# Two more token tiles transposed by the DMA queue, and a new written order for the first stage of a fused adaLN, linear attention and GLU kernel

## The chip, the cores and the metric

The kernel runs on one core of a Trainium2 chip. It is written for five instruction streams: PE (TensorE, matmuls and their weight loads), DVE (VectorE), ACT (ScalarE), POOL (GpSimd) and SP (SyncE, which here only issues DMAs). The metric is the device time of one execution in microseconds; the profile gives the span from the first to the last instruction of one profiled execution.

## What is computed

The input x has 2048 tokens of width D = 512; c is one row of 512. In the reference's words, cut short:

```python
mod = (silu(c) @ w_mod)                      # six rows: sa, ca, ga, sb, cb, gb
h = layernorm(x) * (1 + ca) + sa
q, k, v = split(h @ wqkv)                    # 32 heads of 16
phi(t) = concat(softmax(t @ w_phi), softmax(-t @ w_phi))    # per head, 32 features
kv = sum over tokens of phi(k)^T v ;  z = sum over tokens of phi(k)
o = (phi(q) @ kv) / (phi(q) @ z + 1e-6)
x = x + ga * (o @ wo)
h = layernorm(x) * (1 + cb) + sb
x = x + gb * ((sigmoid(h @ w_gate) * (h @ w_up)) @ w_down)  # F = 1376
```

The sum kv needs all 2048 keys before the first numerator phi(q) @ kv can be formed.

## The kernel before

The tokens stand in 16 tiles of 128. Everything before the first numerator is called the first stage here, everything from it on the second.

**First stage, per tile t.** `st1_t` (DVE, L702 and L703) takes mean and variance of a tile of x. `rs1_g` (ACT or POOL) and `nmr1_g` (DVE, L718) make the scale and shift for the tiles of a group g; `LG` lists the groups: tiles 0 and 1 alone, then pairs, so group 4 is tiles 6 and 7, and group 5 is tiles 8 and 9. `xn1_t` (POOL L731, ACT L727, DVE L729) writes the normalised tile in bf16. It must then be transposed, in four blocks of 128 features, and modulated with the columns of `modc` (1 + ca, sa). There are two ways:

- `TD[g] = 0`: PE transposes the block into a PSUM bank (`tph` with group and block, L744, into the tile named tp_h), and `hm1` with group and block (L751 on ACT, L753 on DVE) reads PSUM and writes the block of `h1T`. POOL has no part in this way.
- `TD[g] = 1`: SP issues a DMA transpose for each tile (`xT1_t`, L736) straight into `h1T`, and `hm1` modulates it in place on ACT, POOL or DVE.

Then `K` (L817), `V` (L821) and `Q` (L871) are matmuls of four 128x512 pieces each; K of the first 8 and V of the first 4 tiles are split in halves a and b. K and Q use `wqk_f`, weights with w_phi folded in (`tpw`, `wTc`, `fold`, `foldc`), V uses `wv_sb`, loaded by the one DMA `ld_wv0` (L551). Per key tile follow `e` (ACT, exponentials, L776), `n` (DVE, sums, L780), `r` (reciprocal: DVE L798, or ACT as logarithm and exponential, L794 and L795), `phi` (POOL or DVE, L787), `va` (ACT, L836) and `kv` (PE, L282, accumulates over all tiles). Query tiles have `qe`, `qn`, `qphi` and a DMA transpose `pT` likewise. At the end `kvz`, `kvn` (DVE, L299 and L294) mask the sums and `num0a` (PE, L326) is the first numerator.

**Second stage.** Per tile: numerators, reciprocal, output projection (a_ps), second LayerNorm, then gate, up and down projections (g_ps, u_ps, y_ps) in chunks of up to four tiles.

**What sets the order.** The schedule is manual. A long string `ORDER` names every task once; the instructions of each engine are issued in the order in which its tasks stand there, and every engine and the SP queue work in order. A letter behind `@` picks the engine (A for ACT, P for POOL, D for DVE); without one, the first of the task's list stands, which for `hm1` is DVE with `TD = 0` and ACT with `TD = 1`, for `r` and `qphi` DVE, for `foldc` ACT, for `phi` POOL. Buffers (8 PSUM banks, 7 slots for e and phi, and so on) are handed out in the same order, so a new order also changes who waits for whose buffer.

## Time and profile before

| | |
|---|---|
| three timed runs | 202.9, 204.34 and 409.55 us; median 204.34 us |
| the profiled execution | 203.25 us; span 201.3 us; granted TensorE clock 1.00 |
| busy: PE, DVE, ACT, POOL | 193.6, 160.0, 104.9, 103.9 us |
| first numerator (num0a) starts | 56.5 us |
| bytes read and written in HBM | 11.58 and 2.10 MB |

One of the three runs took twice the time of the others, so the median is the higher of the two that agree. The profiled execution lies between these two; 1.95 us of it are outside the span. In the profile, times count from the start of the span, and PE matmuls are shown with their pipeline, so that neighbouring rows overlap: what PE takes for a piece of work is read from start to start.

### The profile page before, as it was taken

How to read it: one execution, taken by the hardware profiler on the slowest of the kernel's cores; microseconds unless marked ns; L12 is line 12 of the kernel's file. 1: busy time of each engine (PE TensorE's matmuls, PEld its weight loads, DVE VectorE, ACT ScalarE, POOL GpSimd, SP SyncE). 2: the span in 40 equal slices, each digit the busy share in tenths (PEclk: the TensorE clock that was granted, in tenths of full speed). 3: DMA queues.
4: the chain of work that ended last, by engine and by line, in shares of the span. 5: the costliest groups of instructions: out<-in, count | busy, mean ns of one | idle time of the engine just before them, and what ended most of it. 6: DMA issues, size and time to landing. Idle time of an engine off the chain costs nothing.

```text
span 201.3 us, 4128 instructions
## 1 busy us (share of the span) xinstructions
PE 193.6 (96%) x1447; PEld 106.1 (53%) x1471; DVE 160.0 (79%) x376; ACT 104.9 (52%) x250; POOL 103.9 (52%) x146
## 2 busy tenths in 40 slices
PE   7889999999999999999999999999999999999993
PEld 2555665455565777668744444444444444444442
DVE  3999999999999999997997796875969662326632
ACT  2899999999978974486621215312112420334100
POOL 4889978887899998876660166130030332000000
PEclk9999999999999999999999999999999999999999
DMA  5999956729964883455573334442113031000011
GB/s 163 336 292 236 295 204 126 113 62 268 396 248 78 133 111 68 85 34 105 104 80 80 70 62 102 84 110 56 25 25 74 2 78 55 26 8 26 28 55 55
DMA packets 49453, 22.94 MB, mean 114 GB/s; under 512 B 38065, under 2 KB 47634, under 8 KB 49426
## 3 DMA queue, kind: packets, MB, share of 16 engines
q1 hardware_dynamic: 48896, 22.59, 48.8%
q8 instruction: 13, 0.21, 0.4%
q14 instruction: 14, 0.11, 0.2%
q10 hardware_dynamic: 530, 0.02, 0.1%
HBM read 11.58 MB, written 2.10 MB: 68 GB/s over the span
## 4 chain that ended last, share of the span: by engine, by line
PE 64%; DVE 26%; issue 5%; ACT 2%; DMA 1%; DVEq 0%
PE y_ps L485 19%; PE u_ps L447 18%; PE g_ps L447 18%; DVE ks L780 6%; PE a_ps L356 5%; DVE st L702 5%; DVE qks L780 3%; DVE phi L787 3%; DVE kr L798 2%; PE num L326 2%; DVE h1T L753 2%; DMA x_sb<-in_A_x_dram 1%; DVE mv L703 1%; PE g_ps L449 1%; DVE nmr L718 1%
## 5 line engine op out<-in xcount | busy, mean ns | idle before, releaser
L457 ACT ACTIVATE tg<-g_ps 128x512 bf16<-128x512 f32 (+5 forms) x66 | 28.7, 455 | 66.6 <-PE g_ps L447 39.7
L468 DVE SCALAR_TENSOR_TENSOR wmod_sb<-tg,u_ps 128x512 bf16<-128x512 bf16 (+4 forms) x63 | 30.2, 491 | 18.1 <-ACT tg L457 11.5
L485 PE MATMUL y_ps<-wd_sb,wmod_sb 128*128 128x512 bf16 (+4 forms) x180 | 44.2, 366 | 0.2
L447 PEld LDWEIGHTS <-wg_sb 128*128 128x128 bf16 (+1 forms) x252 | 21.9, 99 | 16.1 <-issue 0.2
L447 PEld LDWEIGHTS <-wu_sb 128*128 128x128 bf16 (+1 forms) x252 | 21.7, 99 | 15.9 <-issue 0.2
L784 POOL TENSOR_TENSOR qphi<-qe,qks 128x512 bf16<-128x512 bf16 x24 | 25.2, 1066 | 3.9 <-DMA pT<-qphi 1.6
L485 PEld LDWEIGHTS <-wmod_sb 128*128 128x128 bf16 (+1 forms) x187 | 17.1, 98 | 16.0 <-issue 0.6
L447 PE MATMUL u_ps<-wT_sb,wu_sb 128*128 128x512 bf16 (+2 forms) x124 | 23.8, 322 | 0.1
L447 PE MATMUL g_ps<-wT_sb,wg_sb 128*128 128x512 bf16 (+2 forms) x122 | 23.0, 321 | 0.2
L447 PE MATMUL g_ps<-wqk_sb,wg_sb 128*128 128x128 bf16 (+4 forms) x127 | 19.9, 286 | 0.1
L447 PE MATMUL u_ps<-wqk_sb,wu_sb 128*128 128x128 bf16 (+4 forms) x127 | 19.8, 286 | 0.1
L492 DVE TENSOR_TENSOR ot<-y_ps,x 128x512 bf16<-128x512 f32 (+2 forms) x17 | 11.1, 654 | 10.4 <-PE y_ps L485 10.3
L780 DVE TENSOR_REDUCE ks<-e 128x64 f32<-128x1024 bf16 (+2 forms) x22 | 19.2, 901 | 0.0
L780 DVE TENSOR_REDUCE qks<-qe 128x64 bf16<-128x1024 bf16 x16 | 19.1, 1202 | 0.0
L376 POOL TENSOR_SCALAR ve<-mv 128x2 f32<-128x2 f32 (+1 forms) x8 | 1.8, 225 | 33.3 <-DVE mv L366 33.2
L776 ACT ACTIVATE e<-k_ps 128x512 bf16<-128x512 f32 (+2 forms) x44 | 18.2, 519 | 0.0
L776 ACT ACTIVATE qe<-q_ps 128x512 bf16<-128x512 f32 x32 | 17.0, 611 | 0.8 <-POOL phi L787 0.5
L817 PE MATMUL k_ps<-wqk_f,h1T 128*128 128x512 bf16 x61 | 16.0, 379 | 0.1
L787 POOL TENSOR_TENSOR phi<-e,kr 128x1024 bf16<-128x1024 bf16 (+2 forms) x10 | 14.8, 1484 | 2.6 <-DVE phi L787 1.2
L356 PE MATMUL a_ps<-wo_sb,oT 128*128 128x512 bf16 x60 | 15.9, 379 | 0.2
L871 PE MATMUL q_ps<-wqk_f,h1T 128*128 128x512 bf16 x61 | 15.7, 379 | 0.1
L821 PE MATMUL v_ps<-wv_sb,h1T 128*128 128x512 bf16 x61 | 15.4, 379 | 0.1
(132 smaller groups left out, 305.6 us busy)
## 6 DMA issues: line engine op xcount, KB each, us to landing
out_dram<-ot SPq DMA_DIRECT2D x15, 128.0 KB, 1.7
x_sb<-in_A_x_dram SPq DMA_DIRECT2D x6, 256.0 KB, 4.7
wmod_sb<-in_w_mod_dram SPq DMA_DIRECT2D x1, 1536.0 KB, 7.0
wu_sb<-in_B_w_up_dram SPq DMA_DIRECT2D x1, 1376.0 KB, 11.5
wg_sb<-in_B_w_gate_dram SPq DMA_DIRECT2D x1, 1376.0 KB, 11.9
wd_sb<-in_B_w_down_dram SPq DMA_DIRECT2D x1, 1280.0 KB, 8.5
wmod_sb<-in_w_mod_dram SPq DMA_DIRECT2D x4, 256.0 KB, 6.1
wqk_sb<-in_A_wqkv_dram SPq DMA_DIRECT2D x2, 256.0 KB, 4.4
```

Of the source, the lines that this page charges most:

```text
L356: pe.matmul(ap_[:], lhsT=oT[:, j, :], rhs=wo_sb[:, j, :], start=(j == 0), stop=(j == KT - 1))
L447: pe.matmul(ps[:fsz, 0:n], lhsT=w[:, j, ft * P:ft * P + fsz], rhs=h[:, j, 0:n], start=(j == 0), stop=(j == KT - 1))
L457: G.add(f"tg{k}.{ft}", {"ACT": 0.13 + n * 0.00083}, lambda e, tg=tg, g_ps=g_ps, fsz=fsz, n=n: act.activation(tg[:fsz, 0:n], g_ps[:fsz, 0:n ...
L468: dve.scalar_tensor_tensor(hm_all[:fsz, hm[k].slot, ft, 0:n], tg[:fsz, 0:n], 1.0, u_ps[:fsz, 0:n], op0=ALU.add, op1=ALU.mult)
L485: mm = pe.matmul(y[:, 0:c1 - c0], lhsT=hm_all[:fsz, hm[k].slot, ft, tl * P:(tl + 1) * P], rhs=wd_sb[:fsz, ft, c0:c1], start=(ft == 0), sto ...
L776: act.activation(ee[:, a:b, s].rearrange("p g f h -> p g (f h)"), kp[:, a * 64:b * 64].rearrange("p (g n) -> p g n", n=64), ACT.Exp, scale ...
L780: dve.tensor_reduce(ks[:, a:b].rearrange("p g s h -> p (g s) h"), ee[:, a:b].rearrange("p g s f h -> p (g s) h f"), axis=AX.X, op=ALU.add)
L784: engine(e).tensor_tensor(ph[:].rearrange("p (g s f h) -> p g s f h", s=2, f=DH, h=4)[:, :, s], ee[:, :, s], ks[:, :, 1 - s].unsqueeze(2). ...
L787: engine(e).tensor_tensor(ph[:, a * P:b * P].rearrange("p (g f h) -> p g f h", f=DH, h=4), ee[:, a:b].rearrange("p g s f h -> p (g s) f h" ...
L817: pe.matmul(kp[:], lhsT=h1T[:, j, t * P:(t + 1) * P], rhs=wqk_f[:, j, D:2 * D], start=(j == 0), stop=(j == KT - 1))
L821: pe.matmul(vp[:], lhsT=h1T[:, j, t * P:(t + 1) * P], rhs=wv_sb[:, j, :], start=(j == 0), stop=(j == KT - 1))
L871: pe.matmul(qp[:], lhsT=h1T[:, j, t * P:(t + 1) * P], rhs=wqk_f[:, j, 0:D], start=(j == 0), stop=(j == KT - 1))
```

## The change

Two things change, and both lie in the first stage. Group 5 (tiles 8 and 9) gets `TD = 1`: its eight PE transposes into four PSUM banks go, two DMA transposes `xT1_8` and `xT1_9` on SP come, and of its four modulated blocks two move to POOL (`hm1_51@P`, `hm1_52@P`) and two go to ACT. And the part of `ORDER` ahead of `num0a` is written anew, with other engines for some tasks; from `num0a` on, the string is the same word for word. The SP queue keeps the order of its first 23 DMAs, up to the loads of the other modulation weights and of wo; xT1_9 and xT1_8 come behind these. The diff, cut to the table and to the first lines of the string:

```diff
-TD = [0, 0, 0, 0, 0, 0, 1, 1, 0]
+TD = [0, 0, 0, 0, 0, 1, 1, 1, 0]
...
-hm1_00@A tph02 hm1_23 rs1_6@P hm1_13@A hm1_02 nmr1_3 st1_9 st1_8 xn1_5 tph03 K0a tph41 hm1_03@A tph40 xn1_4 K2a hm1_22@A hm1_12@A hm1_41@A hm1_40 wqT1 nmr1_6
...
+hm1_20@A K3a modc1c1 nmr1_3 hm1_03@A st1_10 hm1_41 V0a st1_9 hm1_02@A xn1_5 tph42 tph43 wqT3 tph23 hm1_12@A hm1_13@A rs1_6@P hm1_42 xn1_4 nmr1_6 xn1_10 st1_8
...
```

Tasks of the first stage that change their engine (beside group 5):

| from | to | tasks |
|---|---|---|
| ACT | DVE | hm1_01, hm1_41, hm1_42, foldc01, r0, r2, r4, r5, r7, the second half of r14 |
| DVE | ACT | hm1_02, hm1_23, hm1_33, hm1_81, r1, r6, r8, modc1c1 |
| POOL | DVE | one half of qphi0, one half of qphi4, a quarter of phi11 |
| DVE | POOL | phi3, a quarter of phi11 |
| ACT, POOL | the other of the two | xn1_3 (to POOL), rs1_3 and hm1_72 (to ACT) |

**PE, where the first matmul with the V weights stands.** In the rows, `LDWEIGHTS` loads a block, v_ps is the result of V, k_ps that of K, tp_h a transposed block; the first V is V0a, tile 0. Before, the rows around it are the last three pieces of K of tile 1, V0a, and one transposed pair of group 4:

```order
L817 MATMUL k_ps_434<-wqk_f_67,h1T_73 128x512
L817 LDWEIGHTS h1T_73
L817 MATMUL k_ps_434<-wqk_f_67,h1T_73 128x512
L821 LDWEIGHTS h1T_73
L821 MATMUL v_ps_461<-wv_sb_66,h1T_73 128x512
L821 LDWEIGHTS h1T_73
L821 MATMUL v_ps_461<-wv_sb_66,h1T_73 128x512
L744 LDWEIGHTS xn_321
L744 MATMUL tp_h_468<-ident_75,xn_321 128x128
```

Now on PE, at the same V0a, a half of K of tile 3 stands ahead of it, and two blocks of group 4 (tp_h_375 is the one of `tph42`) behind it:

```order
L817 MATMUL k_ps_356<-wqk_f_67,h1T_73 128x512
L817 LDWEIGHTS h1T_73
L817 MATMUL k_ps_356<-wqk_f_67,h1T_73 128x512
L821 LDWEIGHTS h1T_73
L821 MATMUL v_ps_367<-wv_sb_66,h1T_73 128x512
L821 LDWEIGHTS h1T_73
L821 MATMUL v_ps_367<-wv_sb_66,h1T_73 128x512
L744 LDWEIGHTS xn_348
L744 MATMUL tp_h_375<-ident_75,xn_348 128x128
L744 LDWEIGHTS xn_322
L744 MATMUL tp_h_375<-ident_75,xn_322 128x128
```

V0a has moved forward past six halves of K (of tiles 0 to 3), one fold and eight pairs of transposes, among them the block of `tph42`, which now stands right behind it.

**DVE, in the middle of the statistics.** BN_STATS and BN_AGGR are one `st1`; h1T<-tp_h is an `hm1` from PSUM, nmr an `nmr1`. Before, from `modc1c1` to the twelfth `st1` and the block `hm1_40`:

```order
L638 TENSOR_TENSOR modc_78<-modc_ps_332,mone_80 128x2x2
L753 TENSOR_SCALAR h1T_73<-tp_h_309,modc_78 128x256
L753 TENSOR_SCALAR h1T_73<-tp_h_355,modc_78 128x128
L718 TENSOR_SCALAR nmr_89<-mv1_82,rs1_84 128x1 x2
L702 BN_STATS st1_81<-x_sb_65 128x6
L703 BN_AGGR mv1_82<-st1_81 128x2
L702 BN_STATS st1_81<-x_sb_65 128x6
L703 BN_AGGR mv1_82<-st1_81 128x2
L753 TENSOR_SCALAR h1T_73<-tp_h_379,modc_78 128x256
```

Now on DVE, from the second `nmr1` pair of the same stretch to the one behind `hm1_42`, which reads tp_h_375:

```order
L718 TENSOR_SCALAR nmr_89<-mv1_82,rs1_84 128x1 x2
L702 BN_STATS st1_81<-x_sb_65 128x6
L703 BN_AGGR mv1_82<-st1_81 128x2
L753 TENSOR_SCALAR h1T_73<-tp_h_350,modc_78 128x256
L702 BN_STATS st1_81<-x_sb_65 128x6
L703 BN_AGGR mv1_82<-st1_81 128x2
L753 TENSOR_SCALAR h1T_73<-tp_h_375,modc_78 128x256
L718 TENSOR_SCALAR nmr_89<-mv1_82,rs1_84 128x1 x2
```

Two blocks of group 4 that ACT modulated are DVE's now; the second stands on DVE behind eleven `st1`, where before `hm1_40` stood behind twelve, and it reads a PSUM block that PE writes behind V0a.

## The prediction

> **What bounds the kernel now.** I looked first at the page, then at the busy time of the engines in four stretches: the start, the first stage up to the last key work, the passage to the second stage, and the rest.

> ```profile
> PE 193.6 (96%) x1447; PEld 106.1 (53%) x1471; DVE 160.0 (79%) x376; ACT 104.9 (52%) x250; POOL 103.9 (52%) x146
> ...
> core 0: us, PE busy (x) PEld busy (x) DVE busy (x) ACT busy (x) POOL busy (x), PEclk, DMA share, GB/s
> 0.00:12.60 12.60, 10.21 (x85) 5.17 (x86) 9.18 (x31) 8.34 (x21) 8.57 (x30) 1.00 0.94 258
> 12.60:55.90 43.30, 42.79 (x405) 24.16 (x413) 42.98 (x88) 42.25 (x116) 37.80 (x44) 1.00 0.85 219
> 55.90:67.30 11.40, 10.97 (x98) 6.18 (x98) 11.37 (x33) 9.96 (x20) 11.24 (x11) 1.00 0.54 148
> 67.30:201.30 134.00, 129.63 (x869) 70.60 (x881) 96.46 (x227) 44.30 (x97) 46.31 (x64) 1.00 0.34 63
> ```

> After 67.3 us PE is the bound, with 129.6 of 134.0 us. In the first stage the average hides that PE, DVE and ACT are all full: from 12.6 to 55.9 us DVE works 42.98 of 43.30 us, PE 42.79, ACT 42.25. DVE has no idle time to give back, and it also ends the stage:

> ```profile
> 56.47 0.97 PE L326 MATMUL num<-kvb,pT 128*128 128x68 bf16 x24 [0.33 <-DVE kvb L294]
> ...
> 63.80 0.81 ACT xn L400
> ...
> 67.76 0.38 PE u_ps L447 x4
> ```

> The first numerator waits for DVE's kvb, and the chain that ended last stays on DVE, with small stops, until ACT takes over at 63.8, and it reaches PE at 67.8, whose order from here on is unchanged and dense. So what comes later at 56.5 us should come later at the end by about as much. The question is only when DVE reaches kvb, and the order on PE and DVE before it.

> **The change, part by part: work.** The prices are the means in ns behind the busy time, picked from the groups of lines up to 57 us, the last row from those up to 67 us:

> ```profile
> L798 DVE RECIPROCAL kr<-ks 128x64 bf16<-128x64 f32 x4 | 2.1, 536 | 0.0
> L798 DVE RECIPROCAL kr<-ks 128x32 bf16<-128x32 f32 x4 | 1.3, 330 | 0.0
> L753 DVE TENSOR_SCALAR h1T<-tp_h,modc 128x256 bf16<-128x256 bf16 x8 | 3.1, 400 | 0.0
> L753 DVE TENSOR_SCALAR h1T<-tp_h,modc 128x128 bf16<-128x128 bf16 x2 | 0.7, 335 | 0.0
> L784 DVE TENSOR_TENSOR qphi<-qe,qks 128x512 bf16<-128x512 bf16 x3 | 1.2, 417 | 0.0
> L787 DVE TENSOR_TENSOR phi<-e,kr 128x1024 bf16<-128x1024 bf16 x7 | 4.6, 678 | 0.0
> L638 DVE TENSOR_TENSOR modc<-modc_ps,mone 128x4 f32<-128x4 f32 x1 | 0.1, 129 | 0.0
> L361 DVE TENSOR_TENSOR x<-a_ps,x_sb 128x512 f32<-128x512 f32 x3 | 2.0, 681 | 0.0
> ```

> DVE gets five reciprocals of 64 (2.68 us), one of 32 (0.33), two wide and one narrow hm1 (0.80 and 0.34), two halves of qphi (0.83), and foldc01, which DVE does not do in this trace: it copies 128x512 float32 values from PSUM. The nearest rows are the hm1 of half the width, 0.40, and the sum over 128x512 float32 values from PSUM, 0.68; I take 0.65, near the row of the same size. Together 5.63 us. DVE loses three reciprocals (1.61), five wide hm1, two of them group 5's (2.00), one narrow (0.34), phi3 (0.68) and modc1c1 (0.13): 4.76 us. The quarter of phi11 that it takes and the one that it gives cancel. The difference is 0.87 us, or 0.6 to 0.9 with foldc01 at its bounds; I take **0.8 us more for DVE before kvb**. Nothing hides it, DVE being full.

> The other engines get less or the same. PE loses eight transposes. POOL takes phi3, xn1_3 and two hm1, gives two halves of qphi, hm1_72 and rs1_3, which by its own rows comes out even; ACT gives twelve tasks of all kinds and takes eleven like them. I price these at nothing: from 12.6 to 55.9 POOL has 5.5 us idle, and ACT has no more to do than before. PE's gain is small: eight transposes take from 16.27 to 16.72 in the rows below, 0.45 us, and it only lets PE wait longer for DVE.

> The DMA transposes of tiles 8 and 9 stand on SP behind two large loads:

> ```profile
> 20.41 0.57 SPq L556 DMA_DIRECT2D wmod_sb<-in_w_mod_dram  x1
> 21.04 0.50 SPq L557 DMA_DIRECT2D wo_sb<-in_A_wo_dram  x1
> ...
> 29.29 2.50 SPq L736 DMA_TRANSPOSE h1T<-xn  x2
> ...
> 35.32 1.94 PE L817 MATMUL k_ps<-wqk_f,h1T 128*128 128x512 bf16 x8
> ...
> wmod_sb<-in_w_mod_dram SPq DMA_DIRECT2D x1, 1536.0 KB, 7.0
> ...
> h1T<-xn SPq DMA_TRANSPOSE x4, 3.1
> ```

> The first load lands at 27.4; the second, a third of its size, perhaps at 29. Four transposes, of tiles 9, 12, 8 and 13, then take 1.25 us each on SP: if they wait in the queue, they land by 34 at the latest; if not, at about 26. The eight K matmuls from 35.32 are those of tiles 9 and 8; they keep their place on PE, which the wait below moves back by some 2 us. Before them two blocks each on ACT and POOL have to be done. I price all this at nothing; its cover is 3 us or more, and a landing later than 34 would be paid on PE one for one.

> **The change, part by part: a wait.** V0a moves forward on PE, but the load that it needs does not move on SP:

> ```profile
> 10.22 0.57 SPq L537 DMA_DIRECT2D x_sb<-in_A_x_dram  x1
> 10.84 0.51 SPq L551 DMA_DIRECT2D wv_sb<-in_A_wqkv_dram  x1
> ...
> x_sb<-in_A_x_dram SPq DMA_DIRECT2D x1, 512.0 KB, 5.0
> ...
> 0.00:16.00 16.00, 13.55 (x122) 7.31 (x124) 12.44 (x42) 11.74 (x29) 11.88 (x35) 1.00 0.96 268
> 16.00:17.00 1.00, 1.00 (x13) 0.70 (x11) 1.00 (x4) 1.00 (x3) 0.92 (x3) 1.00 1.27 298
> 17.00:18.00 1.00, 1.00 (x6) 0.43 (x5) 0.96 (x6) 1.00 (x3) 1.00 (x3) 1.00 2.13 34
> ```

> When does wv land? No instruction waited for it, so its landing isn't given. Up to it SP issues twelve loads of 256 KB and two of 512 KB, 4.19 MB, and one DMA transpose of a weight block (0.13 MB) among them: 4.32 MB. At 268 GB/s the queues moved 4.29 MB by 16 us, and 0.30 more in the next, so 4.32 is reached at 16.1; with two more such transposes, issued right behind, at 17.0, where the rate falls to 34 GB/s. The x load issued 0.6 us ahead of it, of the same size, landed at 15.2. I take **16.6**, between 16.1 and 17.0.

> When does PE reach V0a?

> ```profile
> 12.58 0.55 PE L630 MATMUL modc_ps<-sc_bf,wmod_sb 128*128 128x1 bf16 x16 [0.46 <-DMA wmod_sb<-in_w_mod_dram]
> 12.99 0.38 PE L817 MATMUL k_ps<-wqk_f,h1T 128*128 128x512 bf16 x1
> ...
> 16.27 0.61 PE L744 MATMUL tp_h<-ident,xn 128*128 128x128 bf16 x8
> 16.72 1.03 PE L817 MATMUL k_ps<-wqk_f,h1T 128*128 128x512 bf16 x4
> 17.59 0.38 PE L821 MATMUL v_ps<-wv_sb,h1T 128*128 128x512 bf16 x1
> ```

> The modulation matmuls wait until 12.58 for a load whose place on SP is unchanged. From there the new order has these (0.41, to the next row), one pair of transposes (0.11, a quarter of the eight from 16.27 to 16.72) and half of K3 (0.43, half of the four from 16.72 to 17.59) ahead of V0a: PE is there at 13.5, and **waits about 3.1 us**. Before, V0a came at 17.59, behind 3.7 us of work that now stands behind it (six halves of K, a fold, eight pairs of transposes). Queued behind V0a is the transpose for hm1_42, and behind that the rest of groups 2 and 4, V0b and K0b; so DVE waits at hm1_42, and ACT at hm1_23. When is DVE at hm1_42?

> ```profile
> 4.42 0.66 DVE L702 BATCH_NORM_STATS2 st<-x_sb 128x6 f32<-128x512 bf16 x1
> ...
> 5.22 0.66 DVE L702 BATCH_NORM_STATS2 st<-x_sb 128x6 f32<-128x512 bf16 x1
> ...
> 15.82 0.38 DVE L753 TENSOR_SCALAR h1T<-tp_h,modc 128x256 bf16<-128x256 bf16 x1
> ```

> The row at 15.82 is hm1_40. DVE had done the same by then as it will have done at hm1_42, but for one st1 more, 0.80 us from start to start, and modc1c1, 0.13: so DVE is at hm1_42 at 14.9. V0a from 16.6 takes 0.43, the two transposes and their way through PSUM 0.3: hm1_42 starts at 17.3. **DVE stands still for 2.4 us** (1.9 to 2.8 with the bounds of the landing), which it can't make good. What is late next: PE. From V0a to the end of the key work it needed 17.59 to 55.9, 38.3 us; with the 3.7 us moved behind and 0.45 less, from 16.6 it is done at 58.2, ahead of DVE's 56.5 + 0.8 + 2.4 = 59.7. ACT loses as much at hm1_23 as DVE at hm1_42, and had less to do.

> **The sum.** 0.8 + 2.4 = 3.2 us, on the profiled execution's 203.25 us: 206.4 us. Its bounds, 0.6 + 1.9 and 0.9 + 2.8, give 205.7 to 206.9. The profiled execution lies between the two runs of before that agree, 202.9 and 204.34, so I take it as the base; a median may fall some 0.7 us to either side, and this case's own range is 205.2 to 207.5.

> **The rivals.**

> *No wait for wv.* If wv lands by 13.6, V0a runs at once and only DVE's 0.8 us is left: 204.0. For it speaks the fastest load of x, 2.8 us after its issue:

> ```profile
> DMA to landing us min/median/max: 2.8/4.9/5.9
> ```

> Against it speak the bytes ahead of it, and the 5.0 us of its neighbour. [...]

> *PE's clock falls in the wait.* PE stands for 3 us where before it never stood for more than 0.5 after the start. The first matmuls of the trace show a slower PE:

> ```profile
> 1.25 2.74 PE L600 MATMUL warm<-wd_sb 128*128 128x512 bf16 x6 [1.25 <-DVE wd_sb L593]
> ...
> 4.11 2.15 PE L600 MATMUL warm<-wd_sb 128*128 128x512 bf16 x8
> ```

> Six take 2.7 us, 0.45 each, eight of the same take 2.15, 0.27 each or less. If PE comes out of the wait as slow as it starts, for as long as it then was (2.7 us), it loses about 1.4 us at a point where K0 and the first exponentials hang on it, and DVE loses as much again: 207.9, or 209.3 if it stays slow twice as long. It decides whether the wait is long enough, and no row here shows how long that is. [...]

> *Not slower: PE sets the stage, not DVE.* PE is as full as DVE from 12.6 on, so DVE's rows may hide waits for PE, and its 0.8 us may fit into them. If also wv is there in time, the stage gets shorter by the transposes' 0.45 us: 202.8. Against it: DVE shows neither idle time nor longer instructions there, and kvb ends after PE's kv work.

> **How the numbers follow.** The wait for wv with PE at full clock: 0.62. No wait: 0.16. Clock falls: 0.14. Not slower: 0.08. For 8 in 10 the range takes the forecast's own range, the second case with the spread of the runs (203.4 and up) and the lower half of the third: 203.4 to 208.3. A change of 2% is 4.1 us of the median 204.34, about what a measurement of this kernel can tell from none: below 200.3 nothing here leads but mishap, 0.03; above 208.4 the upper half of the third case and the tail of the first, 0.14; between, 0.83.

> **What the profile after would show.** V0a's row on PE with an idle time of 2.6 to 3.5 us before it, released by the DMA of wv_sb, at 16.1 to 17.0; a DVE row of hm1 from tp_h at about 17.3 behind 2 to 3 us idle; no further idle time of DVE until kvb; the first numerator at 59 to 60; from 67 us on the same rows as before, some 3 us later. If V0a has no idle time before it, my landing is wrong; if the numerator is late and the end is not, PE had slack after it; if matmuls behind V0a take 0.4 us from start to start, it was the clock.

## The result, and the profile after

The change made the kernel slower: 211.26 us (209.63 to 211.73, 5 runs) against 204.34, a ratio of 1.036 with an interval of 1.032 to 1.040. Forecast were 206.4 us and a range up to 208.3. The profiled execution took 211.52 us, its span is 209.8.

From the page after, the busy time of the engines over the span, and the granted clock in 40 slices of 5.2 us:

```profile
PE 196.4 (94%) x1440; PEld 106.5 (51%) x1463; DVE 162.8 (78%) x377; ACT 105.4 (50%) x248; POOL 104.7 (50%) x145
...
PEclk9995899999999999999999999999999999999999
```

PE and VectorE have each 2.8 us more of busy time, and the fourth slice has half the clock. In the stretches around it (the columns are those of the prediction's first table: the stretch and its length, PE, PEld, DVE, ACT, POOL, then the clock, the DMA share and GB/s):

```profile
13.00:16.00 3.00, 1.13 (x20) 0.62 (x20) 1.95 (x6) 2.21 (x8) 2.49 (x5) 1.00 0.96 289
16.00:18.00 2.00, 0.63 (x2) 0.29 (x3) 0.00 (x0) 0.00 (x0) 0.00 (x0) 0.50 1.19 305
18.00:20.00 2.00, 2.00 (x12) 1.27 (x11) 1.26 (x5) 0.56 (x1) 0.60 (x1) 0.50 0.92 260
20.00:22.00 2.00, 2.00 (x9) 0.92 (x8) 1.69 (x5) 1.50 (x3) 1.82 (x4) 0.50 0.02 4
22.00:24.00 2.00, 1.95 (x12) 1.18 (x12) 1.43 (x5) 1.18 (x3) 1.62 (x4) 0.79 0.34 66
```

In the profiled execution of the kernel before, the clock stood at 1.00 from 4.65 us to the end of the work. Now all engines stand together from 16 us, and PE then runs at half its clock up to 22.8 us. The four executions without a profile lost clock too: the mean granted clock over the span is 0.984 (two of them and the profiled one) or 0.992 (the other two), and 3.4 us at half clock take 0.008 from it. The timeline of PE, from K3a through V0a to the first numerator, shows where this begins; the bracket is the idle time ahead of a row and what ended it:

```profile
13.53 0.61 PE L817 MATMUL k_ps<-wqk_f,h1T 128*128 128x512 bf16 x2
17.37 1.01 PE L821 MATMUL v_ps<-wv_sb,h1T 128*128 128x512 bf16 x2 [3.24 <-DMA wv_sb<-in_A_wqkv_dram]
18.18 0.85 PE L744 MATMUL tp_h<-ident,xn 128*128 128x128 bf16 x6
...
64.65 0.92 PE L326 MATMUL num<-kvb,pT 128*128 128x68 bf16 x24 [0.42 <-DVE kvb L294]
```

K3a's two matmuls at full clock take 0.6; the two of V0a take 1.01, and 0.81 from their start to that of the next row. The first numerator comes at 64.65 instead of 56.47, 8.18 us later, and from there to the end of the span it is 145.15 us where it was 144.83. So nearly all of the loss lies ahead of 64.65, and there VectorE tells it. The brackets below are all of its stops there of more than 0.1 us:

```profile
14.84 0.18 DVE L703 BATCH_NORM_AGGREGATE mv<-st 128x2 f32<-128x6 f32 x1
18.71 0.41 DVE L753 TENSOR_SCALAR h1T<-tp_h,modc 128x256 bf16<-128x256 bf16 x1 [3.69 <-PE tp_h L744]
...
22.48 0.41 DVE L753 TENSOR_SCALAR h1T<-tp_h,modc 128x256 bf16<-128x256 bf16 x1 [0.71 <-PE tp_h L744]
...
24.96 1.22 DVE L780 TENSOR_REDUCE ks<-e 128x64 f32<-128x1024 bf16 x1 [1.02 <-ACT e L776]
```

Together 5.42 us, all of them before 25 us. A second part is no idle time and so in no list of waits: two products take several times their usual length (0.38 to 0.42 us for one of 512 columns, 0.298 for one of 256). Beside each VectorE row stands GpSimd's row of the same moment:

```profile
36.70 1.19 DVE L784 TENSOR_TENSOR qphi<-qe,qks 128x512 bf16<-128x512 bf16 x1
...
36.55 1.06 POOL L784 TENSOR_TENSOR qphi<-qe,qks 128x512 bf16<-128x512 bf16 x1
...
55.38 1.19 DVE L787 TENSOR_TENSOR phi<-e,kr 128x256 bf16<-128x256 bf16 x1
...
55.26 1.16 POOL L851 TENSOR_TENSOR wo_sb<-wo_sb,ga_sb 128x512 bf16<-128x512 bf16 x1
```

Each VectorE product began 0.12 to 0.15 us after GpSimd's and ended 0.15 to 0.28 us behind it: in effect it waited, and then ran. I call this *stretch*, and count for each run what VectorE's products phi and qphi (both inputs in SBUF) take up to the first numerator beyond 0.298, 0.378 and 0.678 us for 256, 512 and 1024 columns, where it is more than 0.06 us: 1.70 us here, 0.08 before.

The account: 5.42 (stops) + 1.62 (stretch) = 7.04 of 8.18. Of the other 1.14, 0.42 are a later start (the modulation matmuls of `modc1.1` run at 13.00 instead of 12.58) and 0.7 are VectorE's additional work: its instructions up to the first numerator take 63.44 us in sum instead of 61.16, and 1.62 of these 2.28 us are the stretch.

### The profile page after: what moved, and what is told of

Its sections match the earlier page's. It is cut to its first block, busy times and chain, and to the rows that moved or that the text cites. A ratio compares the mean times of both kernels' runs of the same rounds, so it can differ in the third digit from the quotient of the medians.

```text
span 209.8 us, 4111 instructions
## 1 busy us (share of the span) xinstructions
PE 196.4 (94%) x1440; PEld 106.5 (51%) x1463; DVE 162.8 (78%) x377; ACT 105.4 (50%) x248; POOL 104.7 (50%) x145
## 4 chain that ended last, share of the span: by engine, by line
PE 71%; DVE 8%; ACT 6%; SPq 5%; DMA 4%; issue 3%; POOL 1%; DVEq 0%; ACTq 0%; POOLq 0%
PE y_ps L485 17%; PE u_ps L447 16%; PE g_ps L447 16%; PE k_ps L817 5%; PE v_ps L821 5%; PE a_ps L356 4%; DMA wv_sb<-in_A_wqkv_dram 3%; DVE qks L780 3%; ACT qe L776 2%; PE num L326 2%; SPq L537 2%; SPq L542 2%; PE g_ps L449 1%; DVE phi L787 1%; DMA wqk_sb<-xn 1%
## 5 line engine op out<-in xcount | busy, mean ns | idle before, releaser
L447 PEld LDWEIGHTS <-wg_sb 128*128 128x128 bf16 (+1 forms) x252 | 21.9, 99 | 16.5 <-issue 0.5
L447 PEld LDWEIGHTS <-wu_sb 128*128 128x128 bf16 (+1 forms) x252 | 21.7, 99 | 15.9 <-issue 0.3
L784 POOL TENSOR_TENSOR qphi<-qe,qks 128x512 bf16<-128x512 bf16 x22 | 22.9, 1060 | 4.2 <-ACT vaug L836 2.0
L447 PE MATMUL u_ps<-wT_sb,wu_sb 128*128 128x512 bf16 (+2 forms) x124 | 23.8, 322 | 0.1
L447 PE MATMUL g_ps<-wT_sb,wg_sb 128*128 128x512 bf16 (+2 forms) x122 | 23.0, 321 | 0.2
L821 PE MATMUL v_ps<-wv_sb,h1T 128*128 128x512 bf16 x62 | 17.6, 403 | 3.3 <-DMA wv_sb<-in_A_wqkv_dram 3.2
L447 PE MATMUL g_ps<-wqk_sb,wg_sb 128*128 128x128 bf16 (+4 forms) x127 | 19.9, 287 | 0.4 <-POOL wqk_sb L424 0.3
L447 PE MATMUL u_ps<-wqk_sb,wu_sb 128*128 128x128 bf16 (+4 forms) x127 | 19.7, 286 | 0.2
L787 POOL TENSOR_TENSOR phi<-e,kr 128x1024 bf16<-128x1024 bf16 (+2 forms) x11 | 17.7, 1612 | 4.4 <-issue 1.8
L817 PE MATMUL k_ps<-wqk_f,h1T 128*128 128x512 bf16 x61 | 16.6, 391 | 0.1
## 6 DMA issues: line engine op xcount, KB each, us to landing
wmod_sb<-in_w_mod_dram SPq DMA_DIRECT2D x1, 1536.0 KB, 7.1
```

The source lines that it names most:

```text
L447: pe.matmul(ps[:fsz, 0:n], lhsT=w[:, j, ft * P:ft * P + fsz], rhs=h[:, j, 0:n], start=(j == 0), stop=(j == KT - 1))
L784: engine(e).tensor_tensor(ph[:].rearrange("p (g s f h) -> p g s f h", s=2, f=DH, h=4)[:, :, s], ee[:, :, s], ks[:, :, 1 - s].unsqueeze(2). ...
L787: engine(e).tensor_tensor(ph[:, a * P:b * P].rearrange("p (g f h) -> p g f h", f=DH, h=4), ee[:, a:b].rearrange("p g s f h -> p (g s) f h" ...
L817: pe.matmul(kp[:], lhsT=h1T[:, j, t * P:(t + 1) * P], rhs=wqk_f[:, j, D:2 * D], start=(j == 0), stop=(j == KT - 1))
L821: pe.matmul(vp[:], lhsT=h1T[:, j, t * P:(t + 1) * P], rhs=wv_sb[:, j, :], start=(j == 0), stop=(j == KT - 1))
```

## The experiments

The table holds all runs: time and ratio to before with its interval, the start of the first numerator, the sum of VectorE's stops of 0.15 us or more from 12 us to there, its stretch, and the rest, which is the numerator's delay against 56.47 less the stops and less the stretch over 0.08. They follow in groups by their question, not in the order in which they ran.

| kernel | us | ratio | numerator | stops | stretch | rest |
|---|---|---|---|---|---|---|
| before | 204.34 | 1 | 56.47 | 0 | 0.08 | 0 |
| after | 211.26 | 1.032 to 1.040 | 64.65 | 5.42 | 1.70 | 1.14 |
| e1_v_later | 208.72 | 1.015 to 1.029 | 61.62 | 2.85 | 1.08 | 1.30 |
| e2_wv_early | 210.68 | 1.024 to 1.037 | 64.63 | 5.76 | 1.08 | 1.40 |
| e3_fill | 212.48 | 1.034 to 1.045 | 65.61 | 7.11 | 1.08 | 1.03 |
| e4_td_alone | 205.81 | 1.007 to 1.014 | 59.43 | 1.25 | 2.05 | -0.26 |
| e5_v_fwd | 209.66 | 1.021 to 1.038 | 63.14 | 3.93 | 1.83 | 0.99 |
| e6_both | 205.87 | 1.006 to 1.014 | 59.20 | 0.41 | 1.30 | 1.10 |
| e7_both_port | 205.30 | 1.004 to 1.011 | 58.20 | 0.45 | 0.71 | 0.65 |
| e8_port | 210.89 | 1.024 to 1.041 | 64.44 | 6.51 | 0.55 | 0.99 |
| e9_t_ahead | 211.00 | 1.027 to 1.041 | 64.40 | 5.10 | 1.71 | 1.20 |
| e10_fill_t_ahead | 211.55 | 1.026 to 1.042 | 65.29 | 5.95 | 1.80 | 1.15 |
| e11_best_a | 205.85 | 1.006 to 1.013 | 58.43 | 1.42 | 0.50 | 0.12 |
| e12_best_b | 212.99 | 1.040 to 1.050 | 65.75 | 2.84 | 6.42 | 0.10 |
| e13_v_fwd_fill | 207.45 | 1.012 to 1.024 | 60.38 | 3.07 | 0.08 | 0.84 |
| e14_td_t | 206.34 | 1.010 to 1.020 | 59.69 | 2.34 | 1.19 | -0.23 |
| e15_fill_t_m | 208.83 | 1.019 to 1.031 | 61.89 | 3.04 | 1.78 | 0.68 |
| e16_td_t_port | 211.17 | 1.030 to 1.040 | 63.66 | 4.24 | 3.11 | -0.08 |
| e17_td_t2 | 206.41 | 1.012 to 1.020 | 59.61 | 2.42 | 1.18 | -0.38 |
| e18_fill_one | 212.82 | 1.039 to 1.051 | 65.79 | 6.49 | 1.69 | 1.22 |

The profiled execution stands behind the last four columns, all executions behind the times. The rest is 1.0 to 1.4 in most kernels with the new order, 0.65 and 0.12 where work was taken off VectorE (e7, e11), 0.68 in e15, 0.99 and 0.84 in e5 and e13, which have before's order and a later start, and -0.4 to 0.1 in the others with before's order, which have two modulated blocks fewer on VectorE. Stops and stretch carry most of the differences between runs.

### Taking the wait for wv away

**e1_v_later**: the changed kernel with the first v matmuls where nothing is missing for them.

Edits of the written order are shown as the words that move, from left to right as they stand there.

```diff
-... hm1_41 V0a ... V0b hm1_23@A ... K0b fold01 V1a ... va0 wqT2 K3b tph31 V1b V2a ... V2b
+... hm1_41 ... K0b fold01 ... tph33 V0a V0b va0 V1a V1b ... V2a V2b
```

> The changed kernel, with the V matmuls of tiles 0 and 1 (and the first half of tile 2) moved behind K0b, K3b and the transposes of groups 2 to 4 on PE, and the copy va0 behind e0; nothing else is moved. Theory (V0a waits for the load of wv, PE falls to half clock in that wait, and DVE stands still behind it): PE reaches V0a at about 16.4, waits 1 us or less, the granted clock stays at 1.00, DVE has less than 1 us idle between 12.6 us and the first numerator, which starts at 58 to 59.5; 204.5 to 206.5 us. Rival (the loss comes with the DMA transposes of tiles 8 and 9 and the work moved between engines, the wait is covered): the wait goes and the time stays above 209.

208.72 us: 2.5 us of the loss went, less than expected. V0a's wait is gone, but VectorE still stands, later:

```profile
29.57 2.35 DVE L780 TENSOR_REDUCE qks<-qe 128x64 bf16<-128x1024 bf16 x2 [0.42 <-ACT qe L776]
34.42 1.22 DVE L780 TENSOR_REDUCE qks<-qe 128x64 bf16<-128x1024 bf16 x1 [1.04 <-POOL qphi L784]
42.07 3.47 DVE L780 TENSOR_REDUCE ks<-e 128x64 f32<-128x1024 bf16 x3 [1.12 <-ACT e L776]
```

and what it stands for goes back to the DMA transposes of tiles 8 and 9. First the line that issues transposes, from 22 us on (four instructions, with their times to landing), then ScalarE's first block of these tiles in the timeline:

```profile
L736 SPq DMA_TRANSPOSE h1T<-xn x4: 1258/1694/2432, 22.1 to 28.1; - x4
...
DMA to landing us min/median/max: 5.6/6.8/8.2
```

```profile
32.74 0.60 ACT L751 ACTIVATE h1T<-h1T,modc 128x256 bf16<-128x256 bf16 x1 [1.24 <-DMA h1T<-xn]
```

That holds for the stops at 34 and 42 us; those at 25 and 29.6, 0.69 us together, come before it. PE waits there as well (1.33 us), and the clock falls to 0.50 from 33.5 to 36.9 us, so part of this second loss is the clock's again: the one execution of four with a clock of 1.00 took 207.42 us.

The transposes stand on SP behind loads of 1536 and 512 KB. In the changed kernel the same transposes landed at 33.6 and 35.3, but ScalarE came to them at 36.21, and nobody waited.

**e2_wv_early**: the load of wv issued earlier on SP.

```diff
-... ld_x2a wTc2 ... ld_x3a hm1_11@A xn1_7 rs1_3 ld_wv0 K0a
+... ld_x2a ld_wv0 wTc2 ... ld_x3a hm1_11@A xn1_7 rs1_3 K0a
```

> The changed kernel with one DMA moved: the load of wv is issued two places earlier on SP, ahead of the first DMA transpose of a weight block and of the last x load. The order of PE, DVE, ACT and POOL is that of the changed kernel. Theory: wv lands about 2 us earlier, at 15 to 15.5, V0a waits about 1.3 us, the clock stays at 1.00, hm1_42 on DVE waits about 1 us; the last x load lands 1.5 us later, at about 17.3, which costs DVE at most 0.5 us: 205 to 207 us. Rival as before: above 209. A mixed outcome, the wait shorter but the clock still lower, would give 208 to 210.

210.68 us, where 205 to 207 was expected. PE's wait at V0a fell from 3.24 to 1.06 us, VectorE's stop there from 3.69 to 1.03, but then ScalarE and GpSimd waited 2.4 and 2.7 us for the transposes, the clock fell to 0.50 from 34.6 to 41.4 us, and VectorE lost 2.19 and 2.54 us. Not a test of the load's price, then, but the same second wait.

**e5_v_fwd**: the other way round, only this step of the change in the kernel before.

```diff
-... tph03 K0a tph41 ... nmr1_6 ld_x3a ... hm1_42@A K0b K3b e0.0 ld_wv0 ... V0a ... V0b
+... tph03 wqT1 ld_x3a ld_wv0 V0a K0a tph41 ... hm1_42@A V0b K0b K3b e0.0
```

(The DMAs only move in the text; their order on SP is unchanged.)

> The kernel before with one thing of the change: the first two v matmuls (V0a) stand ahead of K0a on PE, where nothing but their weight wv is missing, and V0b behind hm1_42; nothing else moves (the transposes of tiles 8 and 9 stay on PE). PE comes there at about 14.2 us, wv lands near 17.0 (issued at 10.84 in before, 6.1 us from issue to landing in the changed kernel). Theory (the wait for wv, and the clock that falls in it, cost the changed kernel 5.4 us of standing VectorE): PE waits 2.5 to 3 us, the clock falls below 1.0 just behind it, VectorE stands 2.5 to 5 us before 30 us, and the time is 207 to 209.5. Rival (before's order has slack that takes it up, the loss belongs to the change as a whole): under 205.5.

209.66 us, 2.9% over before (interval 2.1 to 3.8): moving one piece of V forward is enough for most of the loss, though 1.75 us of its numerator's delay are stretch (see below). PE waited 2.17 us. The timeline of PE and of VectorE there, and then the stretches, as above:

```profile
16.33 0.59 PE L821 MATMUL v_ps<-wv_sb,h1T 128*128 128x512 bf16 x2 [2.17 <-DMA wv_sb<-in_A_wqkv_dram]
...
17.61 0.41 DVE L753 TENSOR_SCALAR h1T<-tp_h,modc 128x256 bf16<-128x256 bf16 x1 [1.19 <-PE tp_h L744]
21.89 0.41 DVE L753 TENSOR_SCALAR h1T<-tp_h,modc 128x256 bf16<-128x256 bf16 x1 [2.59 <-PE tp_h L744]
```

```profile
17.00:17.50 0.50, 0.50 (x7) 0.38 (x6) 0.00 (x0) 0.00 (x0) 0.50 (x1) 1.00 0.94 307
17.50:18.00 0.50, 0.50 (x4) 0.16 (x2) 0.39 (x2) 0.50 (x1) 0.02 (x1) 0.50 1.09 344
18.00:20.50 2.50, 2.50 (x11) 1.24 (x10) 1.27 (x7) 1.11 (x3) 2.07 (x3) 0.50 0.85 83
```

V0a itself ran at full clock. The clock fell 1.1 us after PE had begun to work again, and the larger stop, 2.59 us, lies behind that fall, not at the wait.

### The transposes behind the loads

**e6_both**: e1 with the transposes of tiles 9 and 8 ahead of the two loads on SP.

```diff
-... ld_wmm2 r3.0 va3 ld_wo K4a ... xT1_9 ... xT1_12 phi2.0@D qe1.0 nmr1_8 xn1_14 Q2 xT1_8
+... xT1_9 xT1_8 ld_wmm2 r3.0 va3 ld_wo K4a ... xT1_12 phi2.0@D qe1.0 nmr1_8 xn1_14 Q2
```

> The changed kernel with V0a, V0b, va0, V1a, V1b behind tph33 as in e1_v_later, and with the DMA transposes of tiles 9 and 8 issued ahead of the loads of wmod (1536 KB) and wo (512 KB) instead of behind them. In e1_v_later they were issued at 22.1 and 25.6 us, landed 8.2 and 7.0 us later, and PE and VectorE then waited for the modulated blocks: VectorE stood 2.85 us in four places. Theory (the transposes were late because 2 MB of loads lay ahead of them): they are issued at about 21 and 22, land in 3 to 4.5 us, VectorE's idle time falls from 2.85 to under 0.7, the first numerator comes at about 59 instead of 61.62, and the time is 205.2 to 206.6 against 208.7. Rival (a DMA transpose beside other traffic takes 7 us wherever it stands, or the blocks were late for another reason): 208 or more.

205.87 us, as expected. SP issues the four transposes in a row, the loads behind them, and one small stop of VectorE is left:

```profile
18.34 5.14 SPq L736 DMA_TRANSPOSE h1T<-xn  x4
23.54 0.58 SPq L556 DMA_DIRECT2D wmod_sb<-in_w_mod_dram  x1
...
29.39 2.35 DVE L780 TENSOR_REDUCE qks<-qe 128x64 bf16<-128x1024 bf16 x2 [0.41 <-ACT qe L776]
```

The stops go from 2.85 to 0.41 and the time by 2.85. The late transposes cost that much, once V0a's wait is out of their way, and the clock that falls behind them is part of it; in e6 it stays at 1.00.

**e9_t_ahead**: the same move in the changed kernel, V0a left where it is (the diff is that of e6 alone).

> The changed kernel with only the DMA transposes of tiles 9 and 8 moved ahead of the loads of wmod and wo on SP's queue; V0a still waits for wv. In the changed kernel these transposes landed at 33.5 and 35.3 us and ScalarE reached the first block made of them at 36.21, with no wait: the late landing was covered by the 5.4 us that VectorE had lost before. Theory (two losses of which the first hides the second): no idle time to take away, 210.5 to 211.7 as the changed kernel's 211.26. Rival (the late transposes hold something back in the changed kernel too): 209.5 or less.

211.00 us: no gain that the noise would show, as expected. In the changed kernel itself the late transposes cost nothing that can be measured, because the first wait had made everybody else later still. Two losses of some 3 us, of which the first hides the second.

### The clock

**e3_fill**: PE kept at work in the wait, by 15 matmuls of zeros into V0a's bank, which V0a overwrites.

```diff
         def f_v(e, js=range(KT), t=t, vp=vp):
+            for _ in range(15 if t == 0 and js[0] == 0 else 0):
+                pe.matmul(vp[:], lhsT=wd_sb[:, FT - 1, 0:P], rhs=wd_sb[:, FT - 1, :], start=True, stop=True)
             for j in js:
```

> The changed kernel with 15 matmuls over a block of zeros put ahead of V0a on PE, 0.216 us each at full clock, into the bank that V0a then overwrites; they need nothing that is late, so they fill the wait for wv without shortening it. This parts the wait from the clock. Theory: V0a still starts at 17.2 to 17.5, DVE still stands 3.0 us at hm1_42, but the granted clock is 1.00 and the matmuls behind V0a take 0.216 us; the idle time of DVE behind hm1_42 (0.7 and 1.0 us) goes, and 0.7 us at hm1_42 itself: 208 to 209 us. If the clock has no part in the loss: 211, as the changed kernel.

212.48 us, more than either case expected. The clock stayed at 1.00 up to 37.6 us and VectorE stood 2.84 us at V0a instead of 3.69, 0.71 and 1.02. But then it stood 3.13 and 1.14 us behind transposes that landed at 36.6, and the clock fell from 37.6 to 41.0: the gain went into the wait that e1 shows.

**e10_fill_t_ahead**: e3 with the transposes ahead of the loads, as in e6.

> e3_fill (15 matmuls of zeros ahead of V0a, so that PE runs on while wv is on its way and the clock stays at 1.00 behind it) with the DMA transposes of tiles 9 and 8 ahead of the loads. In e3_fill VectorE stood 2.84 us at V0a, and then 3.13 and 1.14 us behind transposes that landed at 36.6. Theory: the 2.84 stay, the 4.27 go to under 0.7, and the time is 208.4 to 209.4 against 212.48; against e9_t_ahead the 2.6 us between 5.42 and 2.84 are the price of the clock that falls in the wait. Rival (matmuls of zeros don't save what the clock takes, or the second wait returns): 210.5 or more.

211.55 us, and so the rival, at first sight. But the load of wmod was now behind the transposes, PE waited 1.79 us for it at the modulation matmuls `modc2`, the clock fell to 0.50 there (34.7 to 41.5 us), and VectorE stood 2.98 us up to 45.6. One of the four executions kept its clock at 1.00: it took 209.35 us, in the range of the theory; the others had 0.979 to 0.992 and took 211.00 to 212.49.

**e15_fill_t_m**: e10 with `modc2` moved behind K6b.

```diff
-... xn1_15 modc2.0 tph81 ... tph80 modc2.1 qphi0.0 Q4 hm1_80@A modc2c ... hm1_50 K6b
+... xn1_15 tph81 ... tph80 qphi0.0 Q4 hm1_80@A ... hm1_50 K6b modc2.0 modc2.1 modc2c
```

> e10_fill_t_ahead with the three steps modc2, for which PE waited 1.79 us there, behind K6b. Theory: VectorE stands 2.7 to 2.9 us at V0a and under 0.8 after it, the clock is 1.00 from 14 to 60 us, and the time is 208.4 to 209.4: the changed kernel less the 2.6 us that the fallen clock took. Rival (another wait takes the place, or the clock is no part of the loss): 210.5 or more.

208.83 us, as expected. The timeline with the filling, V0a and VectorE's only stop of the stage, and two of the stretches that had the clock at 0.50 in the changed kernel:

```profile
13.91 3.40 PE L821 MATMUL v_ps<-wd_sb 128*128 128x512 bf16 x15
17.21 0.59 PE L823 MATMUL v_ps<-wv_sb,h1T 128*128 128x512 bf16 x2
...
18.02 0.41 DVE L753 TENSOR_SCALAR h1T<-tp_h,modc 128x256 bf16<-128x256 bf16 x1 [3.04 <-PE tp_h L744]
```

```profile
18.00:20.00 2.00, 1.95 (x19) 1.22 (x18) 1.94 (x6) 1.82 (x4) 1.10 (x3) 1.00 0.68 190
20.00:22.00 2.00, 2.00 (x14) 1.01 (x13) 1.93 (x8) 2.00 (x6) 1.92 (x4) 1.00 0.54 141
```

V0a is as late as in the changed kernel, the clock stays, the stops are 3.04 instead of 5.42, and the time is 2.4 us less. Its four executions all have a granted clock of 0.998 or more. As e9 shows that the transposes' move gives nothing by itself, the 2.4 us (2.2 against e9) are the clock's; that the move of `modc2` gives nothing by itself is not shown.

**e13_v_fwd_fill**: e5 with 10 such matmuls ahead of V0a (the diff is that of e3 with 10 for 15).

> e5_v_fwd (the order of before, V0a ahead of K0a, V0b behind hm1_42) with 10 matmuls of zeros ahead of V0a, 0.216 us each, as much as PE waited there (2.17 us); they write V0a's bank and are overwritten by it. In e5_v_fwd VectorE stood 1.19 us at the wait and 2.59 us some 3 us later, when the granted clock was 0.50 between 18 and 20 us. Theory (most of the loss is the clock, not the wait): the 1.19 stay or grow to 1.6, the 2.59 go, the clock is 1.00 from 16 to 22 us, and the time is 206.3 to 207.6 against 209.66. Rival (the wait for wv alone makes the loss, whatever the clock does): 209 or more.

207.45 us, in the expected range, but only in part for the expected reason. In the profiled execution (206.79 us) the clock stayed at 1.00, in the other three it did not (0.989 to 0.992, 207.37 to 207.58 us). In the profile the 2.59 us became 0.92, while the first stop grew from 1.19 to 1.99 (wv came 0.5 us later): 0.86 less in sum. The larger part is stretch, 1.83 in e5 and 0.08 here; see below.

**e18_fill_one**: e15 with 120 matmuls of one column in place of the 15 of 512.

```diff
-            for _ in range(15 if t == 0 and js[0] == 0 else 0):
-                pe.matmul(vp[:], lhsT=wd_sb[:, FT - 1, 0:P], rhs=wd_sb[:, FT - 1, :], start=True, stop=True)
+            for _ in range(120 if t == 0 and js[0] == 0 else 0):
+                pe.matmul(vp[:, 0:1], lhsT=wd_sb[:, FT - 1, 0:P], rhs=wd_sb[:, FT - 1, 0:1], start=True, stop=True)
```

> e15_fill_t_m with 120 matmuls of one column (26 ns each by the row of modc_ps, 0.41 us for 16) ahead of V0a in place of the 15 matmuls of 512 columns of zeros: about the same 3.1 us of PE instructions without a pause over 0.1 us, but with a small part of the columns. Theory (the clock follows how many columns PE works on, not whether it waits): the granted clock falls to 0.50 behind V0a as in the changed kernel, VectorE stands 5 us or more, and the time is 210.3 to 212. Rival (only a pause lets the clock fall): it stays at 1.00, and the time is 208.4 to 209.4 like e15_fill_t_m's 208.83.

The clock fell, and it fell while PE was running without a pause. The filling in the timeline of PE, and two stretches within it:

```profile
13.75 3.14 PE L821 MATMUL v_ps<-wd_sb 128*128 128x1 bf16 x119
```

```profile
16.00:16.40 0.40, 0.40 (x22) 0.40 (x20) 0.00 (x0) 0.00 (x0) 0.00 (x0) 0.97 1.14 287
16.40:16.80 0.40, 0.40 (x19) 0.40 (x16) 0.00 (x0) 0.00 (x0) 0.00 (x0) 0.50 1.41 317
```

So in this pair it is the columns worked on that go with the clock, not the absence of a wait: behind 15 matmuls of 512 columns in 3.40 us it stood at 1.00 (e15), within 119 of one column in 3.14 us it fell to 0.50. The time, 212.82, says less: behind the 119th matmul PE stood 2.32 us with no releaser in the profile, and the cause stays open.

### The stretched products

**e7_both_port**: e6 with one stretched product given to GpSimd.

```diff
-phi11.6@D
+phi11.6@P
```

> e6_both with one 128x256 product more on GpSimd: phi11.6 moved off VectorE. In the changed kernel and in the first three experiments that product took 1.1 to 1.2 us on VectorE instead of 0.298, beginning within 0.2 us after GpSimd had begun the product into wo_sb and ending with it. Theory (VectorE's products with two SBUF inputs wait until GpSimd's running product ends): 0.8 us of stretching and 0.3 of work leave VectorE, and the time is 0.7 to 1.3 us below that of e6_both. Rival (VectorE waits there for data in any case, or the stretch jumps to the next product): within 0.4 of e6_both.

205.30 us against 205.87, and the numerator at 58.20 against 59.20. The time gained 0.6 us, between what the theory and the rival expected, and the two intervals overlap; the numerator came 1.0 us earlier. One stretched product went (0.90 us), the next of its kind was stretched by 0.28 instead.

**e8_port**: both stretched products of the changed kernel given to GpSimd.

```diff
-qphi0.0 ... phi11.6@D
+qphi0.0@P ... phi11.6@P
```

> The changed kernel with only its two stretched VectorE products given to GpSimd: qphi0.0 (1.19 us at 36.70 instead of 0.417) and phi11.6 (1.19 us at 55.38 instead of 0.298). V0a still waits for wv, the DMA transposes stay behind the loads. Theory: VectorE loses 1.7 us of stretching and 0.7 of work, GpSimd gains 1.7 of work in a stage where it stands for more than that; the first numerator comes 1.7 to 2.4 us earlier than 64.65 and the time is 208.9 to 209.8. Rival (GpSimd becomes late, or the stretch hid another wait): 210.6 or more.

210.89 us, the rival, not distinguishable from 211.26. The stretch fell from 1.70 to 0.55, but VectorE stood 2.57 us at 39 us for GpSimd's qphi, behind a late transpose (PE waited 1.49 us for the block made of it), and the clock fell a second time, from 37.1 to 40.5 us. Again a gain that the second wait took.

The clearest view of the stretch is a pair that differs in time alone. e5 and e13 have the same order on VectorE and GpSimd. The last three products before kvb (two of 512, one of 1024 columns, merged into one row) with GpSimd's product of that moment, in the timeline of e5 and then in that of e13:

```profile
59.29 2.25 DVE L787 TENSOR_TENSOR phi<-e,kr 128x512 bf16<-128x512 bf16 x3
...
59.92 1.08 POOL L787 TENSOR_TENSOR phi<-e,kr 128x512 bf16<-128x512 bf16 x1 [0.45 <-ACT kr L795]
```

```profile
57.39 1.39 DVE L787 TENSOR_TENSOR phi<-e,kr 128x512 bf16<-128x512 bf16 x3
...
58.40 1.28 POOL L787 TENSOR_TENSOR phi<-e,kr 128x512 bf16<-128x512 bf16 x1 [0.84 <-ACT kr L795]
```

In e5 GpSimd began at 59.92, 0.09 us before VectorE's third product, which then took 1.53 us. In e13 the third product had begun first: it took its 0.68, and GpSimd's took 1.28 instead of 1.08. In both runs the product that began first took its usual time, and the one that began second took longer. Over all the kept traces the ends agree with this: where a VectorE product was stretched beside a product of GpSimd, it ended 0.15, 0.28 or 0.55 us behind it, for 256, 512 and 1024 columns, whether it had been held for 0.1 or for 1.7 us. Beside an `hm1` block on GpSimd a product was longer too: in the kernel before, the one of 1024 columns at 43.03 took 0.73 us and ended 0.54 us behind the block; in e1 one took 0.94 us instead of 0.678 at 47.0.

**e11_best_a** tried to gain more on this way: foldc01 and r4.0 on ScalarE, qphi0.0 on GpSimd, from e7.

```diff
-foldc01@D ... r4.0 ... qphi0.0 
+foldc01 ... r4.0@A ... qphi0.0@P
```

> e7_both_port with four things off VectorE: the copy foldc01 and the reciprocal r4.0 on ScalarE as in before, and qphi0.0, which took 0.81 instead of 0.38 us there, on GpSimd (a 128x512 product, 1.05 us there); phi11.6 stays on GpSimd. VectorE loses 0.68, 0.54, 0.81 us: 2.0 us in all from a first numerator at 58.20, where before has 56.47. Theory (VectorE's dense work sets the first numerator): 56.2 to 56.8, time 203.4 to 204.6. Rival (ScalarE, which gains 0.9 us and is busy 43.8 of 46 us, or GpSimd becomes the bound, or the stretch jumps to other products): 204.8 to 206.

205.85 us, the rival. 2.0 us left VectorE, all of it ahead of 35.5 us, and yet the sum over e that stands there begins at 35.52 instead of e7's 35.42: the savings had become stops. Two of them in the timeline of VectorE:

```profile
22.15 2.35 DVE L780 TENSOR_REDUCE ks<-e 128x64 f32<-128x1024 bf16 x2 [0.59 <-ACT e L776]
...
33.40 1.22 DVE L780 TENSOR_REDUCE qks<-qe 128x64 bf16<-128x1024 bf16 x1 [0.68 <-POOL qphi L784]
```

ScalarE and GpSimd had no room for more.

### The transposes alone, in the order of before

**e4_td_alone**: tiles 8 and 9 by the DMA queue, the order otherwise that of before.

```diff
-TD = [0, 0, 0, 0, 0, 0, 1, 1, 0]
+TD = [0, 0, 0, 0, 0, 1, 1, 1, 0]
-tph50 tph51 tph52 tph53; hm1_50, hm1_53@A, hm1_51@A, hm1_52 in their places
+ld_wo xT1_9 xT1_8; qe1.0 hm1_53@A hm1_50@A; hm1_51@P hm1_52@P qphi1.1
```

> The kernel before with the table change alone: group 5 is transposed by DMA, its two transposes stand on SP behind the loads of the other modulation weights and of wo, two of its modulated blocks go to POOL (ahead of the two halves of qphi1) and two to ACT (behind qe1); all other tasks keep engine and order. Theory: the DMA path costs nothing, DVE loses two blocks of 0.40 us, PE 0.45 us: the first numerator 0.4 to 0.8 us earlier than before, 202.5 to 204 us against 203.5. Rival: the transposes land too late or load POOL: K of tile 9 waits on PE, and the time is 205 or more.

205.81 us, the rival, 1% over before (0.7 to 1.4): the other part of the change costs by itself too. VectorE stands 1.25 us, for an e that ScalarE had begun late behind a transpose (0.53 us), and has 2.05 us of stretch; it saves 0.8 us of blocks.

Four attempts to take these apart, e14, e17, e12 and e16, all with the transposes ahead of the loads:

```diff
 e14, e17, e12, e16: -ld_wo xT1_9 xT1_8   +xT1_9 xT1_8 ld_wmm2
 e14: modc2.0 modc2.1 modc2c behind K7b;  e17: the same three behind V9
 e12: qphi4.1@P; phi15.4@D ahead of phi12.0; wo0 wo3 behind kvz1
 e16: e14 with qphi4.1@P; qn6.0 ahead of phi12.0; wo0 wo3 behind kvz1
```

> e4_td_alone with the transposes of tiles 9 and 8 ahead of the loads of wmod and wo, and with the three steps modc2 that need that load behind K7b, so that PE doesn't wait for it. The stretched products stay. Theory (two losses, late transposes 1.25 us and stretching 2.05 us): the first goes, 204.3 to 205.0 against 205.81. Rival (the stretch alone makes the loss): 205.4 or more.

> e14_td_t with the three steps modc2 behind V9 instead of behind K7b: ScalarE's wait for them (1.13 us at 34.67) and the 1.9 us that VectorE then stood should both go. Theory (e4_td_alone lost 1.25 us to transposes behind 2 MB of loads and some 1.1 to 2 us to products stretched by alignment): the first part goes, VectorE stands under 0.6 us up to the first numerator, and the time is 204.0 to 205.2 against 205.81 of e4_td_alone. Rival (tiles 8 and 9 by the DMA queue cost something else in this order): 205.5 or more.

> e4_td_alone (the order of before, tiles 8 and 9 transposed by the DMA queue) with the transposes ahead of the loads of wmod and wo, and its three stretched VectorE products freed: qphi4.1 on GpSimd, phi15.4 on VectorE ahead of phi12.0, the products wo0 and wo3 of GpSimd behind kvz1. In e4_td_alone VectorE stood 1.25 us and its products were 2.05 us longer than their usual time. Theory: both go, VectorE has 0.8 us less of modulated blocks than before, and the first numerator comes at 56.0 to 56.8, the time is 203.2 to 204.4. Rival (other products are stretched instead, or GpSimd's later wo products are waited for): 204.8 to 206.

> e14_td_t with its stretched products freed as far as they are known from e4_td_alone: qphi4.1 on GpSimd (it began on VectorE 0.37 us after GpSimd had begun qphi4.0), the sum qn6.0 ahead of phi12.0 on VectorE and GpSimd's products wo0 and wo3 behind kvz1 (phi12.0 began 0.09 us after GpSimd's phi15.4). Theory: 0.8 to 1.7 us below e14_td_t, 203.0 to 204.3, level with or just below before. Rival (the stretch moves to other products when anything moves): no faster than e14_td_t, 204.6 or more.

206.34, 206.41, 212.99 and 211.17 us: none met its theory. In e14 and e17 nobody waits for a transpose any more, but ScalarE waits 1.13 and 2.58 us for the moved `modc2`, and VectorE stands 1.92 and 1.99; in e14 the clock falls as well, to 0.50 from 34.2 to 37.6 us. In e12 PE waits 2.07 us for the load of wmod and the clock falls to 0.50 twice, from 32.3 to 35.7 and from 49.3 to 52.7 us. In e12 and e16 the freed products were replaced by others: the stretch rose to 6.42 and 3.11 us. How the 1% of e4 divides between late transposes and stretch stays open. No kernel of these beats the one before.

## Why the prediction was wrong

- **The bound, and the passage to the end: right.** From the first numerator to the end of the span it takes 0.3 us more than before.
- **VectorE's work, +0.8 us: right.** The rest of 1.14 less the later start of 0.42 is 0.7; foldc01 took 0.68, taken as 0.65.
- **The landing of wv, 16.6: the term was too small.** It was 17.37. The load was issued 0.41 us later than before, at 11.25, and took 6.1 us, not 5.8. PE waited 3.24 us, near the 3.1 forecast only by chance, as it too came 0.6 us later (14.1 instead of 13.5). With the clock held, VectorE's stop is 3.04 us (e15), not 2.4: 0.6 us. Of the 0.73 us counted from V0a's start to `hm1_42`, the 0.3 for two transposes and the way through PSUM stood beside no row; in e15 the whole takes 0.81 (17.21 to 18.02).
- **The clock at full speed: the step that failed.** It was a rival with 0.14 and a fair price (1.5 or 2.9 us; measured 2.4). The sum counted on full speed behind a wait of 3.1 us, though no row showed how long a wait must be, and no run shows a wait of that length with the clock at 1.00 behind it: it fell in or behind waits of 3.19, 3.24, 3.40 and 4.02 us (e8, the changed kernel, e3, e9). It fell behind 2.17 and 1.79 us too (e5, e10), and in e18 behind no wait; in the changed kernel it fell at 16 us, some 2 us after PE's last matmul. It changes in steps of 3.41 us (see the last section), and the error was to look at the wait alone: the step that ended at 16.02 was not idle, PE had worked in it for 1.14 us, on 20 matmuls of which 16, those of `modc1.1`, have one column each. The sign that the prediction named, 0.4 us from start to start behind V0a, is there: 0.81 us for V0a's two.
- **No further idle time until kvb, and products at 0.417: wrong, and a term that was missing.** Two more stops came, 0.71 us at half clock and 1.02 us just behind it, and none after 25 us; and 1.62 us of stretch, which is no idle time. The rows of before show products near their usual length; that their moments merely happened to fit there is what e5 and e13 suggest.
- **The transposes at no cost, cover 3 us, landing by 34: right in its sum by luck, wrong in its ground.** They landed at 33.6 and 35.3 and cost nothing (e9), but only because the first wait had moved their readers to 36.2. Without that wait they cost 2.85 us, the clock behind them included (e1 against e6).
- **The sum.** 3.2 forecast; the profiled runs differ by 8.27. 0.6 more for the landing, 2.4 for the clock and 1.6 for stretch make 7.8; the other 0.5 is about the later start (0.4) and the 0.3 behind the numerator, less the 0.1 by which the work was taken too high and 0.2 of difference outside the spans.

## What to carry to other kernels

Where a matmul is moved ahead of its load, price the half clock behind the wait as well as the wait (here 2.4 us, e15 against the changed kernel), and count the columns of PE's matmuls in the 3.41 us of a step, since the clock fell to 0.50 within 119 matmuls of one column in a row (e18) and stayed at 1.00 with 15 of 512 in their place (e15). In a stage in which VectorE and GpSimd are both full, look at the lengths of VectorE's products as well as at its idle time: here the two that began 0.12 and 0.15 us behind one of GpSimd's took 1.19 us each. And when one wait is removed and the gain is small, look for a second one that it had covered; here keeping PE at work gave nothing (e3, 212.48 us) until the transposes were out of its way (e15, 208.83).
